# Attention and two MLPs on one core: score products in float32 from the loaded rows, and a new order of the attention round

## The chip, the cores and the metric

The kernel runs on one core of a Trainium2 chip. The metric is the time of one execution on the device in microseconds (us); three runs of the kernel before gave 993.02, 993.51 and 996.86, so the median is 993.51.

## The reference

```python
# attention: q, k, v of 4 batches x 8 heads x 576 tokens x 64, f of 4 x 8 x 576
scores = scale * np.matmul(q, k.transpose(0, 1, 3, 2))
cum = np.cumsum(np.log(np.clip(f, 0.0001, 1.0)), axis=-1)
scores = np.where(causal, -1e9, scores + cum[..., :, None] - cum[..., None, :])
attn = np.exp(scores - np.max(scores, axis=-1, keepdims=True))
x = np.matmul(attn / (np.sum(attn, axis=-1, keepdims=True) + 1e-09), v)
# x as 2304 tokens x 512, then two MLPs
h = x @ w_in;  x = (h * np.cos(h)) @ w_out          # 512 -> 2048 -> 512
g = x @ w_gate                                      # 512 -> 1536
x = (g / (1 + np.exp(-g)) * (x @ w_val)) @ w_out2   # 1536 -> 512
```

The weights come as 64-bit floats, and the kernel converts them itself.

## The kernel before, in words

The kernel has an attention stage and then two MLP stages. The change touches attention alone (and the point in it where two products of the first MLP are put ahead).

The 32 heads are worked in 16 pairs. The pair's q and k lie as 128 rows (two heads of 64 dimensions) by 2 x 576 tokens in a tile `raw`, loaded by `load_pair`. Queries are cut into tiles: tile t = 0 to 3 holds 128 queries against their first 128(t+1) keys, for each head; tile 4 holds the last 64 queries of both heads against all 576 keys, with q laid on the diagonal of a block `bd` so that one product serves both. For every pair the order has these operations, named by a letter and the tile (and, where there is one for each head, by a last digit 0 or 1):

- **q0 to q3** (`emit_q`, POOL): q and k rounded to float32r (high part), and what is left (low part), in `xq`. **qb** (`emit_b`, POOL): the blocks `bd` and `sf`.
- **S** (`emit_s`, TensorE): scores. Three products (high x high, low x high, high x low) and one more that adds the decay from `cs`. The two heads use the upper and the lower 64 rows of the array. Pair 0, and pair 1 but for tiles 1 and 4, take one product of the loaded rows instead, in float32, with block `bd0` for pair 0's tile 4. A float32 product is issued as two instructions.
- **M** (`emit_m`, DVE): mask, scale, maximum, from PSUM into `P` (tile 4: `Q`). **E** (`emit_e`, ACT): exponential and row sum.
- **T** (`emit_t`, TensorE): `P` transposed in blocks of 64 into a PSUM tile `t` (two buffers, shared with V). **C** (`emit_c`): that tile copied into `pt`, on ACT or DVE. For groups 0 to 2 the two heads' halves are copied apart, and `CPD` names those that DVE takes.
- **V** (`emit_pv`, TensorE, float32): the product with v, in two halves, 28 instructions. **N** (`emit_n`, DVE): times the reciprocal sums. **xo**: the store of the result to DRAM.
- **r**: the reciprocals of the sums: `ra` (POOL), `rb` (DVE), `rt` (transpose), `rc` (copy on ACT), `rd` (store), `re`, `rf` (loads of the broadcast rows `rs`).
- **w1 to w7** (`w_step`): one weight tile's conversion: w1 ACT, w2 POOL (line 170, a clamp), w3 DVE (line 172, a shift), w4 and w5 DVE (lines 174, 176), w6 POOL (a rounding), w7 POOL (line 115, a subtraction). **wd**, **ld**, **lv** are loads of a weight tile, a pair, and v. **xk** loads and splits the first chunk of MLP input.

`SCH` is the order of a round, written out by hand: an entry such as `V0@3` runs operation V0 of pair n-3 in round n. The rounds n = 0, 1, ... follow each other, and the entries of pairs out of range are left out, so the first and last rounds are partly empty. `in_order` ties each engine to this order: an engine starts nothing before what stands ahead of it on the same engine. `FIRST` gives pairs 0 and 1 another order of score tiles; `AHEAD` moves a few reciprocal steps of pairs 0 and 1. `XH` names the two places where twelve products of the first MLP (`ahead`, `mm_in`, line 253) are put ahead of an attention operation. After the last round the first MLP's loop runs; its input chunk 1 is fetched behind a `gate` (a one-element copy on DVE, line 144).

In PSUM the scores of tiles 0, 2 and 4 share `sA` and those of tiles 1 and 3 `sB` (`SAT`), one buffer each, so a tile's scores wait for the maxima of the one before in the same place.

Of the kernel before, what the change touches and what calls it, by code (L numbers as in the profile page):

```python
# [9 lines left out]
F32 = mybir.dt.float32  # L10
F32R = mybir.dt.float32r
# [7 lines left out]
B, H, S, D = 4, 8, 576, 64  # L19
NH = B * H  # L20
NPAIR = NH // 2
# [8 lines left out]
SA = 15  # L30
LAG = 2
PB = 6
RWB = 3
VTB = 3
PTB = 2
PST = 2
# [5 lines left out]
CHAIN = 1  # L42
WHE = 1

CPD = ("10", "11", "21")
FIRST = {0: "20314", 1: "32041"}
XH = {("T1", NPAIR - 1): 0, ("V0", NPAIR - 1): 1}
SCH = "M21@2 w4@4 M31@2 q2@0 w5@4 N0@4 E30@2 ld@-1 N1@4 S4@1 T1@3 E00@2 re@3 rf@3 q0@0 S1@1 xo@4 wd@2 E01@2 E10@2 M40@1 w6@4 T3@3 E21@2 E31@2 C10@3 S2@1 C11@3 w1@3 ra@2 S0@1 w2@3 q3@0 rb@2 M10@1 M11@1 T2@3 rt@2 C30@3 w3@3 q1@0 qb@0 C21@3 E40@1 T0@2 S3@1 rc@2 C20@3 rd@2 M20@1 M01@1 M00@1 C01@2 M30@1 V0@3 E11@1 V1@3 E20@1 w7@4 lv@2 C00@2 xk@3"
JS = 9
NCH = 96  # L50
NPASS, NQ, NST = 3, 6, 2
# [31 lines left out]
PJ = [0, 576, 1088, 1408, 1024]  # L83
# [14 lines left out]
def body(ctx: ExitStack, tc: tile.TileContext, qk, v, f, w_in, w_out, w_gate, w_val, w_out2, mask_c, ident_c, sel_c, out):  # L98
    nc = tc.nc
    PE, ACT, DVE, POOL, SP = nc.tensor, nc.scalar, nc.vector, nc.gpsimd, nc.sync  # L100
# [13 lines left out]
    def subtract(eng, o, a, b):  # L114
        eng.tensor_tensor(out=o, in0=a, in1=b.bitcast(F32), op=ALU.subtract)  # L115

    def pool_round(o, a):
        POOL.tensor_scalar(out=o, in0=a, scalar1=1.0, scalar2=0.0, op0=ALU.mult, op1=ALU.add)
# [161 lines left out]
    ap1 = actx.enter_context(tc.tile_pool(name="ap1", bufs=1))  # L280
# [3 lines left out]
    aps = actx.enter_context(tc.tile_pool(name="aps", bufs=1))  # L284
# [13 lines left out]
    raws = {}  # L298

    def load_pair(i):  # L300
        raws[i] = aps.tile([128, 2, S], F32, tag="raw", name="raw", bufs=RWB)
        SP.dma_start(out=raws[i], in_=qk[i])
# [7 lines left out]

    Ps = [ap1.tile([128, PW], F32, name=f"P{k}") for k in range(PB)]
    P4s = [ap1.tile([128, 640], F32, name=f"Q{k}") for k in range(PB // 2)]
    bd = [ap1.tile([128, 2, 128], F32R, name=f"bd{k}") for k in range(2)]
    sel = ap1.tile([128, NPAIR, 2], F32R, name="sel")
    sel4s = [ap1.tile([128, 128], F32R, name=f"sf{k}") for k in range(2)]
    bd0 = ap1.tile([128, 128], F32, name="bd0")
    fo, lc = Ps[2:4]
    lf, ones, cum = fo[:, 0:S], fo[:, S:2 * S], lc[:, 0:S]
    cs = aps.tile([128, S], F32R, name="cs")
    selr = aps.tile([128, NPAIR + 1], F32, name="selr")  # L320
    POOL.memset(mask[:, 0:384], 0.0)
    POOL.memset(mask4[:, 0:512], 0.0)
    for b in (bd0, sel, *bd):
        POOL.memset(b.bitcast(F32), 0.0)
    SP.dma_start(out=lf, in_=f)
    load_pair(0)
    SP.dma_start(out=selr, in_=sel_c)
# [32 lines left out]

    SAT = {0: (sA, 384), 1: (sB, 0), 2: (sA, 0), 3: (sB, 0)}

    xq = {}

    def emit_q(i, k):

        if i not in xq:
            xq[i] = aps.tile([128, 2, 2, S], F32R, tag="xq", name="xq", bufs=2)
        h, l, x = xq[i][:, 0, k // 2], xq[i][:, 1, k // 2], raws[i][:, k // 2]
        if k % 2 == 0:  # L370
            pool_round(h, x)
        else:
            subtract(POOL, l, x, h)

    def emit_b(i):
        q = slice(512, S)
        if i == 0:
            for e in range(2):
                b = slice(64 * e, 64 * e + 64)
                pool_round(sel[b, :, e], selr[b, :NPAIR])  # L380
        pool_round(sel4s[i % 2].rearrange("p (e x) -> p e x", e=2), sel[:, i, :, None].bitcast(F32).to_broadcast([128, 2, 64]))
        for e in range(2):
            b = slice(64 * e, 64 * e + 64)
            if i:
                pool_round(bd[i % 2][b, :, b], xq[i][b, :, 0, q].bitcast(F32))
            else:
                pool_round(bd0[b, b], raws[i][b, 0, q])

    early = {}

# [8 lines left out]
        return x[:, :, lo:lo + QT[t][1]]  # L399

    def emit_s(i, t):
        if i > 1 or i == 1 and t in (1, 4):
            xh, xl = xq[i][:, 0], xq[i][:, 1]
            h, l = bd[i % 2][:, 0], bd[i % 2][:, 1]
            p = (xh, xh, h), (xl, xh, l), (xh, xl, h)
        else:
            p = (raws[i], raws[i], bd0),
        if t < 4:
            q0, ext, _ = QT[t]
            o = s_place(i, t)  # L410
            for m, (x, y, _) in enumerate(p):
                for e in range(2):
                    b = slice(64 * e, 64 * e + 64)
                    PE.matmul(o[:, e], lhsT=x[b, 0, q0:q0 + 128], rhs=y[b, 1, :ext], start=(m == 0), stop=False)
            for e in range(2):
                b = slice(64 * e, 64 * e + 64)
                PE.matmul(o[:, e], lhsT=sel[b, i, e:e + 1].to_broadcast([64, 128]), rhs=cs[b, :ext], start=False, stop=True)
            return
        o = s_place(i, 4)
        for m, (x, y) in enumerate([*((x, y) for _, y, x in p), (sel4s[i % 2], None)]):  # L420
            for g in range(2):
                k = slice(288 * g, 288 * g + 288)
                PE.matmul(o[:, g], lhsT=x, rhs=cs[:, k] if y is None else y[:, 1, k], start=(m == 0), stop=(y is None))

    P = {}
    mxt = [ap1.tile([128, 5], F32, name=f"mx{i}") for i in range(8)]
# [65 lines left out]
            for h in range(2):  # L492
                turn(ps[:, h, 64 * n:64 * n + 64], x, h)

    def emit_c(i, g, e):
        if i not in PT:
            PT[i] = ap2.tile([128, 2, PTW], F32, tag="pt", name="pt", bufs=PTB)
        ps, o = tps[i, g], PT[i]

        def copy(o, x):  # L500
            if f"{g}{e}" in CPD or i == 0 and g == 3:
                DVE.tensor_copy(o, x)
            else:
                ACT.copy(out=o, in_=x)  # L504

        n = 4 - g
        if g < 3:
            copy(o[:, e, PJ[g]:PJ[g] + 128 * n].rearrange("p (n h x) -> p n h x", n=n, h=2),
                 ps[:, :, 64 * n * e:64 * n * e + 64 * n].rearrange("p h (n x) -> p n h x", n=n))
            return  # L510
        if g == 3:
            copy(o[:, :, PJ[g]:PJ[g] + 128].rearrange("p e (h x) -> p e h x", h=2), ps[:, :, :128].rearrange("p h (e x) -> p e h x", e=2))
            c = 128
            for js in TAILS:
                a, k = PJ[js[0]] + KW[js[0]] - 64, len(js)
                d = PJ[js[1]] + KW[js[1]] - 64 - a
                copy(o[:, :, a:a + d * (k - 1) + 64].rearrange("p e (j q) -> p e j q", q=64)[:, :, ::d // 64],
                     ps[:, :, c:c + 64 * k].rearrange("p e (j q) -> p e j q", j=k))
                c += 64 * k
# [39 lines left out]
    SLOTS = {k: [t for _, _, t in sorted((int(f), n, t) for n, (t, f) in enumerate(sch) if t[0] == k)] for k in "SME"}  # L559
# [4 lines left out]
    def op(o, i):  # L564

        if not 0 <= i < NPAIR:
            return
        if i in FIRST and o[0] in "SME":
            o = o[0] + flat(o[0], FIRST[i])[SLOTS[o[0]].index(o)]
        if (o, i) in BEHIND:  # L570
# [2 lines left out]
            act(*a)  # L573
        act(o, i)

    AHEAD = {("M10", 1): (("ra", 0), ("rb", 0)), ("C10", 0): (("rt", 0), ("rc", 0), ("rd", 0)), ("T0", 1): (("re", 0), ("rf", 0))}
    BEHIND = {a for b in AHEAD.values() for a in b}

    def act(o, i):
        k, e = o[0], int(o[-1]) if o[-1] in "01" else 0  # L580
        p = 2 * i + e
        if o[:2] == "ld":
            i > 1 and load_pair(i)
        elif o == "lv":
            prep_v(i)
        elif k == "S":
            emit_s(i, int(o[1]))
        elif k == "M":
            emit_m(p, int(o[1]))
        elif k == "E":  # L590
            emit_e(p, int(o[1]))
        elif k == "T":
            emit_t(i, int(o[1]))
        elif k == "C":
            emit_c(i, int(o[1]), e)
        elif k == "r":
            emit_recip(i, o[1])
        elif k == "V":
            emit_pv(i, e)
        elif k == "N":  # L600
            emit_n(i, e)
        elif o == "xo":
            emit_o(i)
        elif o == "xk":
            if i == XL:
                load_chunk(0, True)
            elif i >= XP:
                for _ in range(min(XN, len(xsplit))):
                    split_x(*xsplit.pop(0))
        elif o == "wd":  # L610
            i and w_load(i - 1)
        elif k == "w":
            i and w_step(i - 1, int(o[1]))
        elif o == "qb":
            emit_b(i)
        elif k == "q":
            i and emit_q(i, int(o[1]))
        else:
            raise ValueError(o)

# [18 lines left out]
    for n in range(NPAIR + moff):  # L639
        for o, off in sch:  # L640
            if (o, n - int(off)) in XH:
                ahead(XH[o, n - int(off)])
            op(o, n - int(off))
            if n - int(off) == NPAIR - 1 and o == "C01":
                ACT.activation(out=sinp, in_=hpi, func=AF.Sin)
    in_order(first)
    gsrc[0] = const.tile([1, 1], F32, name="gs")
# [131 lines left out]
    for i in range(NCH + LAG):  # L779
        if i < NCH:  # L780
            g, j = steps[i]
            c, a, b = SEG[g]
# [60 lines left out]
    ps = ctx.enter_context(tc.tile_pool(name="ps", bufs=1, space=PSUM, reuse_waits="tile"))  # L843
# [182 lines left out]
    for st in range(NST):  # L1026
        for p in range(NPASS):
            final = st == NST - 1 and p == NPASS - 1
            for q in range(NQS * st, NQS * st + NQS):
                k = q - NQS * st  # L1030
# [89 lines left out]
```

## Time and profile before

| | |
|---|---|
| median of three runs | 993.51 us |
| the profiled execution's own time | 992.61 us |
| its span, first to last instruction | 990.5 us |
| TensorE (PE) busy | 949.6 us, 96% |
| DVE busy | 747.9 us, 76% |
| ACT busy | 502.2 us, 51% |
| POOL busy | 496.8 us, 50% |
| granted TensorE clock, mean | 0.989 |

The profile is one execution. Busy times are those of instructions that work on data. A matmul's end is modelled, so a busy PE need not be at its peak. The shares are means over the attention stage (0 to about 191 us) and the MLP stages after it.

### The profile page before, as it was taken

The page shows a single profiled execution, that of the slowest core. Times are in us where ns is not written, and L with a number is a line of the kernel's source. Part 1 is how long each engine was busy: PE and PEld are TensorE (multiplying, and loading weights), DVE is VectorE, ACT ScalarE, POOL GpSimd, SP SyncE. Part 2 cuts the span into 40 slices and gives each one's busy share as a digit, 9 for nine tenths or more (in the row PEclk, how much of TensorE's full clock was granted, in tenths as well). Part 3 has the DMA queues.
Part 4 walks back from the last instruction along what each step waited for, and adds up shares of the span by engine and source line. Part 5 has one row for each costly group of instructions (what it writes and reads, how often), then busy time and mean ns, then how long its engine had stood idle before and what let it go on. Part 6 is the DMA issues. An engine that isn't in the chain of part 4 may idle for free.

```text
span 990.5 us, 18044 instructions
## 1 busy us (share of the span) xinstructions
PE 949.6 (96%) x6522; PEld 897.8 (91%) x6522; DVE 747.9 (76%) x1312; ACT 502.2 (51%) x1106; POOL 496.8 (50%) x492
## 2 busy tenths in 40 slices
PE   7898887799999999999999999999999999999998
PEld 4676675699999999999999999999999999988888
DVE  6888987378788878879894744867567686898884
ACT  6787786355555555556655532423233241454552
POOL 6699997352227569679785002644454464200000
PEclk9999998989999999999999999999999999999999
DMA  5565564333356767877856775134951419953431
GB/s 171 185 217 194 187 220 135 136 105 129 94 193 206 243 201 236 268 236 260 278 195 223 258 265 171 48 120 133 341 182 49 127 50 352 347 195 125 147 107 43
DMA packets 108984, 182.60 MB, mean 184 GB/s; under 512 B 8912, under 2 KB 72800, under 8 KB 108896
## 3 DMA queue, kind: packets, MB, share of 16 engines
q1 hardware_dynamic: 108896, 181.46, 55.6%
q8 instruction: 51, 0.84, 0.3%
q14 instruction: 37, 0.30, 0.1%
HBM read 118.43 MB, written 62.99 MB: 183 GB/s over the span
## 4 chain that ended last, share of the span: by engine, by line
PE 72%; DVE 3%; issue 2%; POOL 2%; DMA 1%; ACT 0%; SPq 0%; DVEq 0%; POOLq 0%; ACTq 0%
PE h L253 17%; PE t L699 16%; PE b L890 11%; PE c L890 8%; PE a L890 8%; PE b L979 5%; PE a L979 3%; PE c L979 1%; PE d L979 1%; PE t L702 1%; DVE c L115 1%; DMA xl<-x 1%; POOL sums L115 1%; DVE gs L764 0%; DVE ta L174 0%
## 5 line engine op out<-in xcount | busy, mean ns | idle before, releaser
L253 PE MATMUL h<-xh,w 128*128 128x384 f32 x768 | 150.0, 336 | 0.0
L699 PE MATMUL t<-gh,w 128*128 128x384 f32 x704 | 137.9, 337 | 4.1 <-ACT gh L683 3.5
L253 PEld LDWEIGHTS h<-xh,w 128*128 128x128 f32 x768 | 135.5, 189 | 0.2
L699 PEld LDWEIGHTS t<-gh,w 128*128 128x128 f32 x704 | 124.1, 189 | 5.1 <-ACT gh L683 3.8
L890 PE MATMUL b<-c,wu 128*128 128x384 f32 x648 | 121.1, 334 | 0.0
L675 ACT ACTIVATE n<-h 128x384 int32<-128x384 f32 x96 | 47.2, 491 | 139.9 <-PE h L253 139.7
L890 PEld LDWEIGHTS b<-c,wu 128*128 128x128 f32 x648 | 113.1, 188 | 0.0
L677 DVE SCALAR_TENSOR_TENSOR r<-h,n 128x384 f32<-128x384 f32 x96 | 53.1, 553 | 73.5 <-ACT n L675 73.2
L853 POOL TENSOR_TENSOR s<-u,s 128x384 f32<-128x384 f32 x33 | 37.7, 1144 | 123.7 <-ACT s L852 123.7
L253 PE MATMUL h<-xl,w 128*128 128x384 f32 x384 | 82.0, 334 | 0.0
L890 PE MATMUL c<-c,wu 128*128 128x384 f32 x432 | 80.7, 334 | 0.0
L890 PE MATMUL a<-c,wu 128*128 128x384 f32 x432 | 80.7, 334 | 0.0
L115 POOL TENSOR_TENSOR w<-ta,w 128x512 fp32r<-128x512 f32 x32 | 48.8, 1524 | 62.4 <-DVE ta L172 31.3
L699 PE MATMUL t<-gl,w 128*128 128x384 f32 x352 | 75.8, 336 | 0.0
L890 PEld LDWEIGHTS c<-c,wu 128*128 128x128 f32 x432 | 75.4, 188 | 0.0
L890 PEld LDWEIGHTS a<-c,wu 128*128 128x128 f32 x432 | 75.4, 188 | 0.0
L533 PEld LDWEIGHTS t<-pt,vt 128*64 128x64 f32 x448 | 32.0, 147 | 46.8 <-ACT pt L504 28.6
L533 PE MATMUL t<-pt,vt 128*64 128x320 f32 (+4 forms) x448 | 51.7, 386 | 22.7 <-ACT pt L504 22.6
L446 ACT ACTIVATE P<-P,mx 128x256 f32<-128x256 f32 (+3 forms) x128 | 70.2, 550 | 0.2 <-DVE mx L438 0.2
L253 PEld LDWEIGHTS h<-xl,w 128*128 128x128 f32 x384 | 67.9, 188 | 0.0
L172 DVE TENSOR_SCALAR ta<-ta 128x512 int32<-128x512 int32 x68 | 56.3, 828 | 14.3 <-POOL ta L170 13.8
L679 ACT ACTIVATE r<-r,hpi 128x384 f32<-128x384 f32 x96 | 59.5, 619 | 10.6 <-DVE r L677 10.5
(160 smaller groups left out, 2122.9 us busy)
## 6 DMA issues: line engine op xcount, KB each, us to landing
wu<-wu SPq DMA_DIRECT2D x63, 512.0 KB, 7.7
wraw<-in_w_out_dram SPq DMA_DIRECT2D x28, 512.0 KB, 3.8
wu<-hi SPq DMA_DIRECT2D x54, 256.0 KB, 4.4
gd<-g SPq DMA_DIRECT2D x72, 192.0 KB, 2.3
gt<-gd SPq DMA_DIRECT2D x36, 384.0 KB, 3.9
raw<-in_qk_dram SPq DMA_DIRECT2D x16, 576.0 KB, 4.4
wu<-sums SPq DMA_DIRECT2D x36, 256.0 KB, 4.3
xb<-x SPq DMA_DIRECT2D x24, 384.0 KB, 5.8
```

Source lines behind the costliest of these rows:

```text
L115: eng.tensor_tensor(out=o, in0=a, in1=b.bitcast(F32), op=ALU.subtract)
L172: DVE.tensor_scalar(out=ta, in0=ta, scalar1=5, scalar2=2, op0=ALU.logical_shift_left, op1=ALU.logical_shift_right)
L253: PE.matmul(ps, lhsT=w[:, a, 128 * kk:128 * kk + 128], rhs=b[:, kk], start=(n == 0), stop=(n == 3 * KD - 1))
L446: ACT.activation(out=o, in_=o, func=AF.Exp, scale=-1.0, bias=mxt[p % 8][:, t:t + 1], accum_out=smt[p // 2 % 3][:, c:c + 1])
L533: PE.matmul(ps[64 * e:64 * e + 64, o:min(w, o + KW[j])], lhsT=vt_t[i][:, j, e], rhs=PT[i][:, e, c:c + w - o], start=(j == 0), stop=(j == b ...
L675: ACT.activation(out=n, in_=h, func=AF.Copy, scale=INV2PI, bias=0.25)
L677: DVE.scalar_tensor_tensor(out=r, in0=h, scalar=INV2PI, in1=n, op0=ALU.mult, op1=ALU.subtract)
L679: ACT.activation(out=r, in_=r, func=AF.Sin, bias=hpi, scale=float(2 * np.pi))
L699: PE.matmul(acc[m][:, :CH], lhsT=wo[:, q, 128 * m:128 * m + 128], rhs=x, start=(j == a and n == 0), stop=False)
L853: e.tensor_tensor(out=s, in0=C[:, 0], in1=s, op=ALU.mult)
L890: PE.matmul(d, lhsT=wu[q, i][1][:, mem, x, 128 * kt:128 * kt + 128], rhs=r, start=bool(s and n == 0), stop=(n == 5), skip_group_check=True)
L979: PE.matmul(ot[:, :w], lhsT=cmb[i][:, x, q], rhs=m[:, 256 * y:256 * y + w], start=(i in (1, 5) and n == 0), stop=(n == len(ops) - 1), skip ...
```

## The change

The split of q and k goes (`emit_q`, `xq`, the low and high `bd`): all pairs take one float32 product of the loaded rows for each score tile, and `bd` is now float32, filled from the loaded rows. `emit_c` copies both heads in one operation; DVE takes group 1 (and pair 0's group 3), ACT the rest. The loaded pairs get a fourth buffer (`RWB`). The round has a new order, in which V, N and xo stand at the head of a round with offset 4, and w6, w7 have offset 5; pair 1's order of score tiles, the places of `AHEAD` and `XH` and the place of the sine table's load move with it.

```diff
-RWB = 3
+RWB = 4
...
-CPD = ("10", "11", "21")
-FIRST = {0: "20314", 1: "32041"}
-XH = {("T1", NPAIR - 1): 0, ("V0", NPAIR - 1): 1}
-SCH = "M21@2 w4@4 M31@2 q2@0 w5@4 N0@4 E30@2 ld@-1 N1@4 S4@1 T1@3 E00@2 re@3 rf@3 q0@0 S1@1 xo@4 wd@2 E01@2 E10@2 M40@1 w6@4 T3@3 E21@2 E31@2 C10@3 S2@1 C11@3 w1@3 ra@2 S0@1 w2@3 q3@0 rb@2 M10@1 M11@1 T2@3 rt@2 C30@3 w3@3 q1@0 qb@0 C21@3 E40@1 T0@2 S3@1 rc@2 C20@3 rd@2 M20@1 M01@1 M00@1 C01@2 M30@1 V0@3 E11@1 V1@3 E20@1 w7@4 lv@2 C00@2 xk@3"
+FIRST = {0: "20314", 1: "20341"}
+XH = {("V0", NPAIR - 2): 0, ("V0", NPAIR - 1): 1}
+SCH = "lv@3 E21@2 V0@4 E30@2 V1@4 M31@2 qb@0 w6@5 w4@4 N0@4 N1@4 xo@4 E01@2 C0@3 ld@-1 S4@1 E31@2 S1@1 re@3 rf@3 M40@1 w7@5 T3@3 w5@4 T1@3 ra@2 wd@2 w1@3 M11@1 C3@3 rb@2 M10@1 S0@1 w2@3 C1@3 S2@1 E11@1 T2@3 rt@2 M00@1 E10@1 M21@1 M20@1 w3@3 S3@1 C2@3 rc@2 rd@2 T0@2 M30@1 E00@1 E40@1 E20@1 xk@3 M01@1"
...
-    bd = [ap1.tile([128, 2, 128], F32R, name=f"bd{k}") for k in range(2)]
+    bd = [ap1.tile([128, 128], F32, name=f"bd{k}") for k in range(2)]
...
-    xq = {}
-
-    def emit_q(i, k):
-
-        if i not in xq:
-            xq[i] = aps.tile([128, 2, 2, S], F32R, tag="xq", name="xq", bufs=2)
-        h, l, x = xq[i][:, 0, k // 2], xq[i][:, 1, k // 2], raws[i][:, k // 2]
-        if k % 2 == 0:
-            pool_round(h, x)
-        else:
-            subtract(POOL, l, x, h)
-
...
-            if i:
-                pool_round(bd[i % 2][b, :, b], xq[i][b, :, 0, q].bitcast(F32))
-            else:
-                pool_round(bd0[b, b], raws[i][b, 0, q])
+            pool_round(bd[i % 2][b, b], raws[i][b, 0, q])
...
     def emit_s(i, t):
-        if i > 1 or i == 1 and t in (1, 4):
-            xh, xl = xq[i][:, 0], xq[i][:, 1]
-            h, l = bd[i % 2][:, 0], bd[i % 2][:, 1]
-            p = (xh, xh, h), (xl, xh, l), (xh, xl, h)
-        else:
-            p = (raws[i], raws[i], bd0),
+        x = raws[i]
         if t < 4:
             q0, ext, _ = QT[t]
             o = s_place(i, t)
-            for m, (x, y, _) in enumerate(p):
-                for e in range(2):
-                    b = slice(64 * e, 64 * e + 64)
-                    PE.matmul(o[:, e], lhsT=x[b, 0, q0:q0 + 128], rhs=y[b, 1, :ext], start=(m == 0), stop=False)
+            for e in range(2):
+                b = slice(64 * e, 64 * e + 64)
+                PE.matmul(o[:, e], lhsT=x[b, 0, q0:q0 + 128], rhs=x[b, 1, :ext], start=True, stop=False)
...
-        for m, (x, y) in enumerate([*((x, y) for _, y, x in p), (sel4s[i % 2], None)]):
+        for m in range(2):
             for g in range(2):
                 k = slice(288 * g, 288 * g + 288)
-                PE.matmul(o[:, g], lhsT=x, rhs=cs[:, k] if y is None else y[:, 1, k], start=(m == 0), stop=(y is None))
+                if m:
+                    PE.matmul(o[:, g], lhsT=sel4s[i % 2], rhs=cs[:, k], start=False, stop=True)
+                else:
+                    PE.matmul(o[:, g], lhsT=bd[i % 2], rhs=x[:, 1, k], start=True, stop=False)
...
-    def emit_c(i, g, e):
+    def emit_c(i, g):
...
-            if f"{g}{e}" in CPD or i == 0 and g == 3:
+            if g == 1 or i == 0 and g == 3:
                 DVE.tensor_copy(o, x)
             else:
                 ACT.copy(out=o, in_=x)
 
         n = 4 - g
         if g < 3:
-            copy(o[:, e, PJ[g]:PJ[g] + 128 * n].rearrange("p (n h x) -> p n h x", n=n, h=2),
-                 ps[:, :, 64 * n * e:64 * n * e + 64 * n].rearrange("p h (n x) -> p n h x", n=n))
-            return
+            copy(o[:, :, PJ[g]:PJ[g] + 128 * n].rearrange("p e (n h x) -> p e n h x", n=n, h=2),
+                 ps[:, :, :128 * n].rearrange("p h (e n x) -> p e n h x", n=n, e=2))
...
-    AHEAD = {("M10", 1): (("ra", 0), ("rb", 0)), ("C10", 0): (("rt", 0), ("rc", 0), ("rd", 0)), ("T0", 1): (("re", 0), ("rf", 0))}
+    AHEAD = {("M40", 1): (("ra", 0), ("rb", 0)), ("C3", 0): (("rt", 0), ("rc", 0), ("rd", 0)), ("T2", 0): (("re", 0), ("rf", 0))}
...
-            if n - int(off) == NPAIR - 1 and o == "C01":
+            if n - int(off) == NPAIR - 1 and o == SLOTS["E"][-1]:
                 ACT.activation(out=sinp, in_=hpi, func=AF.Sin)
```

## Rows read from the trace of the kernel before

**Rows 1.** The page, busy us, share of the span and instructions of TensorE.

```profile
PE 949.6 (96%) x6522; PEld 897.8 (91%) x6522; DVE 747.9 (76%) x1312; ACT 502.2 (51%) x1106; POOL 496.8 (50%) x492
```

**Rows 2.** Windows: stretch, length, busy (count) by engine, granted clock, DMA share, GB/s.

```profile
18.29:158.10 139.81, 116.43 (x1562) 92.31 (x1562) 119.84 (x350) 105.74 (x344) 124.49 (x141) 0.98 0.61 199
158.10:191.03 32.93, 27.13 (x302) 21.29 (x299) 21.00 (x51) 17.75 (x49) 17.80 (x18) 0.90 0.36 119
191.03:990.50 799.47, 791.99 (x4579) 776.09 (x4578) 594.86 (x862) 364.89 (x678) 341.24 (x305) 1.00 0.57 186
```

**Rows 3.** Timeline of SP's queue: start, us, result stores of two successive pairs.

```profile
83.34 0.33 SPq L547 DMA_DIRECT2D x<-xp  x1
...
93.79 0.33 SPq L547 DMA_DIRECT2D x<-xp  x1
```

**Rows 4.** Windows: one round, columns PE, PEld, DVE, ACT, POOL as in rows 2.

```profile
83.34:93.79 10.45, 8.60 (x126) 6.91 (x124) 9.32 (x28) 8.07 (x28) 9.95 (x12) 1.00 0.62 201
```

**Rows 5.** Timeline of DVE: start, us, w3 beside a busy and an idle POOL.

```profile
86.80 1.63 DVE L172 TENSOR_SCALAR ta<-ta 128x512 int32<-128x512 int32 x1 [1.13 <-POOL ta L170]
...
183.07 0.41 DVE L172 TENSOR_SCALAR ta<-ta 128x512 int32<-128x512 int32 x1
```

**Rows 6.** Timeline of PE: the first V instructions of a round, idle before.

```profile
89.36 0.87 PE L533 MATMUL t<-pt,vt 128*64 128x256 f32 x8 [1.85 <-ACT pt L504]
```

**Rows 7.** Groups of POOL by form, 50 to 150 us: count, busy us, mean ns, idle.

```profile
L115 POOL TENSOR_TENSOR xq<-raw,xq 128x576 fp32r<-128x576 f32 x18 | 26.6, 1501 | 0.0
...
L118 POOL TENSOR_SCALAR xq<-raw 128x576 fp32r<-128x576 f32 x20 | 17.1, 868 | 0.0
...
L118 POOL TENSOR_SCALAR bd<-xq 64x128 fp32r<-64x128 f32 x18 | 5.3, 294 | 0.7
```

**Rows 8.** Groups of DVE and ACT by form, 50 to 150 us: the copies of transposed scores.

```profile
L502 DVE COPY pt<-t 128x384 f32<-128x384 f32 x20 | 10.1, 544 | 0.0
...
L502 DVE COPY pt<-t 128x256 f32<-128x256 f32 x9 | 3.7, 410 | 0.0
...
L504 ACT COPY pt<-t 128x256 f32<-128x256 f32 x29 | 10.3, 355 | 1.6 <-PE t L483 1.6
L504 ACT COPY pt<-t 128x512 f32<-128x512 f32 x18 | 10.1, 563 | 0.0
```

**Rows 9.** Timeline of PE: tile 4 and tile 3 of a late pair, three rounded products.

```profile
81.75 1.06 PE L423 MATMUL sA<-xq,bd 128*128 128x288 f32 x6
...
82.65 0.42 PE L423 MATMUL sA<-cs,sf 128*128 128x288 f32 x2
...
86.33 0.95 PE L414 MATMUL sB<-xq 64*128 64x512 f32 x6
...
87.12 0.40 PE L417 MATMUL sB<-cs,sel 64*128 64x512 f32 x2
```

**Rows 10.** The same tiles of pairs 0 and 1, one float32 product.

```profile
9.34 1.24 PE L423 MATMUL t<-raw,bd 128*128 128x288 f32 x4
...
10.20 0.64 PE L423 MATMUL t<-cs,sf 128*128 128x288 f32 x2
...
10.78 1.13 PE L414 MATMUL sB<-raw 64*128 64x512 f32 x4
...
11.34 0.80 PE L417 MATMUL sB<-cs,sel 64*128 64x512 f32 x2
```

**Rows 11.** Timeline of PE: three V products, 28 instructions each.

```profile
153.56 4.61 PE L533 MATMUL t<-pt,vt 128*64 128x256 f32 x28 [2.45 <-ACT pt L504]
...
164.09 2.92 PE L533 MATMUL t<-pt,vt 128*64 128x256 f32 x28 [0.20 <-ACT pt L504]
...
174.35 4.47 PE L533 MATMUL t<-pt,vt 128*64 128x256 f32 x28 [2.40 <-ACT pt L504]
```

**Rows 12.** Windows: a stretch of the first MLP, where PE has only rounded 384-column products.

```profile
225.00:250.00 25.00, 25.00 (x146) 25.00 (x145) 21.63 (x40) 14.34 (x30) 5.42 (x4) 1.00 0.40 129
```

**Rows 13.** Timeline of PE: tile 4 of pair 2, idle before.

```profile
18.29 1.06 PE L423 MATMUL sA<-xq,bd 128*128 128x288 f32 x6 [2.61 <-POOL bd L118]
```

**Rows 14.** Timeline of DVE: the gate of the second MLP chunk.

```profile
197.66 0.14 DVE L144 CAST xl<-gs 1x1 fp32r<-1x1 f32 x1 [6.66 <-issue]
```

More of the change, by code (lines that the diff above doesn't have):

```diff
@@ L312, in body @@
     P4s = [ap1.tile([128, 640], F32, name=f"Q{k}") for k in range(PB // 2)]
-    bd = [ap1.tile([128, 2, 128], F32R, name=f"bd{k}") for k in range(2)]
+    bd = [ap1.tile([128, 128], F32, name=f"bd{k}") for k in range(2)]
     sel = ap1.tile([128, NPAIR, 2], F32R, name="sel")
     sel4s = [ap1.tile([128, 128], F32R, name=f"sf{k}") for k in range(2)]
-    bd0 = ap1.tile([128, 128], F32, name="bd0")
     fo, lc = Ps[2:4]
@@ L322, in body @@
     POOL.memset(mask4[:, 0:512], 0.0)
-    for b in (bd0, sel, *bd):
-        POOL.memset(b.bitcast(F32), 0.0)
+    for b in (sel.bitcast(F32), *bd):
+        POOL.memset(b, 0.0)
     SP.dma_start(out=lf, in_=f)
@@ L594, in act @@
         elif k == "C":
-            emit_c(i, int(o[1]), e)
+            emit_c(i, int(o[1]))
         elif k == "r":
@@ L615, in act @@
             emit_b(i)
-        elif k == "q":
-            i and emit_q(i, int(o[1]))
         else:
```

## The prediction

> **What bounds the kernel now.** I first read the page's engine totals: TensorE is busy for 96% of the span [rows 1]. Such a share is a mean over stages, so I cut the span where the stages change. After 191.03 us (the last attention result leaves) TensorE is busy 791.99 of 799.47 us [rows 2]: the two MLPs run at its pace, nothing in the change touches them, and I cost them at nothing. Everything is decided in the 191 us of attention before.
>
> There the work comes in rounds. The stores of the attention results leave 10.45 us apart [rows 3], and in one such round POOL is busy 9.95 us, DVE 9.32, PE 8.60, ACT 8.07 [rows 4]. POOL has half a microsecond left in twelve instructions, which is their own starting time, so POOL sets the round. The others show that they wait for it: DVE idles 1.13 us for POOL's clamp ahead of its shift (w3), that shift then lasts 1.63 us beside POOL's subtractions where it lasts 0.41 us beside an idle POOL [rows 5], the copy behind it comes late, and PE idles 1.85 us for the copies of the transposed scores ahead of the V product [rows 6]. That is one chain: POOL, DVE, ACT, PE.
>
> **The change, part by part.**
>
> *No split of q and k (POOL).* Per round POOL loses two roundings at 0.868 and two subtractions at 1.501 us: 4.74 us [rows 7]. The block for the last 64 queries stays two operations, on 64x64 in place of 64x128 (0.294 us each [rows 7]); I keep their price. POOL falls from 9.95 to 5.2 us a round and cannot pace a round above that. What it slowed gets quicker too: DVE's shift may fall from 1.63 towards 0.41 us [rows 5], but POOL still has its clamp and its weight subtraction each round, so I bound DVE's gain here between 0 and 1.2 us.
>
> *Copies of both heads in one operation.* DVE had two copies of 384 columns and one of 256: 2 x 0.544 + 0.410 = 1.50 us. It keeps one of 768. From 256 to 384 columns a copy grows by 0.134 us [rows 8], so 768 come to 0.544 + 3 x 0.134 = 0.95 us: DVE saves 0.55. ACT had two of 512 and one of 256 (2 x 0.563 + 0.355 = 1.48 us) and gets one of 1024 and one of 512; 256 columns more cost 0.208 us [rows 8], so 0.563 + 2 x 0.208 + 0.563 = 1.54: ACT gains 0.06. No row has the new pattern, which runs over both heads and has one dimension more. By the nearest rows it lies between these sums and the price of the separate copies it joins plus half as much again (DVE +0.7, ACT +0.8); I take the sums, since the inner run stays 64 columns. So DVE goes from 9.32 to 7.6 to 8.8 us a round, ACT from 8.07 to 8.1.
>
> *Scores as float32 products (PE).* Per round three products of rounded parts (six matmuls for a tile) become one float32 product (four instructions for a tile, since float32 is issued as two for each head). Pairs 0 and 1 already do this in the trace, so the same tiles stand there in both forms. Measured from the first start to the last end with the decay product behind it, the last-queries tile took 81.75 to 82.65 + 0.42, so 1.32 us, and in float32 9.34 to 10.20 + 0.64, so 1.50; the 512-column tile 86.33 to 87.12 + 0.40, so 1.19, and in float32 10.78 to 11.34 + 0.80, so 1.36 [rows 9, 10]. That is +0.18 and +0.17. The other three are shorter, where two instructions fewer weigh most: I take nothing for them. Sum +0.35 us a round. The upper end comes from columns alone: the float32 V product runs 1600 columns in 2.92 us, or 1.82 ns a column [rows 11], the MLP's rounded products 384 columns in 25.00/146 = 0.171 us, 0.446 ns a column [rows 12]. The round's 1280 + 576 score columns would go from 3 x 0.446 to 1.82 ns: +0.9 us. The lower end is 0, if fewer instructions win back the columns. So PE needs 8.60 + 0.35 = 8.95 us a round, between 8.6 and 9.5.
>
> In "FP8 and Floating Point Precision", section "TensorE Precision Notes", the Trainium skill says that true FP32 takes four passes through the array; that speaks against this edit, since three products become four passes. The trace agrees on the rate (1.82 against 0.446 ns a column), while the tiles' elapsed times show less than half of the rise. With four passes paid in full the round would be 9.5 us.
>
> *Round laid out anew.* The order decides whether PE really gets to run through. I walked one round by it, with durations from these rows, V starting at 0. V ends at 2.9; the division (DVE) runs to 3.7; the last-queries scores end at 4.4 and their maximum at 5.1; w5, the two 256-column maxima and a reciprocal end at 6.5 to 7.0; ACT's exponentials of these end at 7.5 and its last copy and row copy at about 8.1. Only these hold the next V, and PE itself is busy to 8.95. The shift w3 now stands behind the copy that V needs, so POOL's clamp holds no copy for PE: the 1.85 us [rows 6] go. ACT's own loop, 8.1 us and half a microsecond of wait for the last 512-column maxima, also fits. What is late next is PE itself. I take 9.0 us a round. On SP the pair's load now stands behind the result's store, which waits for the division; it leaves by about 4.5 and is used in the next round. A fourth buffer of loaded rows lets it leave without waiting for readers.
>
> **The sum**, against the profiled execution (span 990.50, time 992.61 us).
> - Middle: from the last-queries scores of pair 2 (18.29) to those of pair 15 (158.10) are 13 rounds and 139.81 us [rows 2]. Thirteen rounds of 10.45 would be 135.9; the remaining 4 us are two V products that ran long, beside a mean granted clock of 0.98 (one took 4.61 in place of 2.92 us, [rows 11]). PE with fewer idle gaps should keep the clock. New: 13 x 9.0 = 117.0. Saved 22.8.
> - Start: pair 2's scores waited 2.61 us for the block that POOL builds from the rounded parts [rows 13]; that block now comes from the loaded rows. The maxima of pair 1 are over by then, so the wait goes whole; the first rounds, still without V, may be a little shorter than 9.0. Saved 3.3 (bounds 1 to 5).
> - End: from 158.10 to the last V product's results, 32.93 us at a granted clock of 0.90 [rows 2], in rounds without score work but with the same chain through w3, and with one more slow V (4.47 us at 174.35, [rows 11]). By the walk: 6 us to end round 16; 8.8 for the next, where the table load for the sine and the exponentials are in ACT's way; about 12.7 to the end of the last V, with two groups of twelve MLP products ahead of it; 1 for division and store. 28.5 us. Saved 4.4 (bounds 1 to 7).
> - Seam: DVE stood idle for 6.66 us until 197.66 [rows 14], after the last store and before the second chunk of MLP input is fetched; that hangs behind the store and moves with it. Nothing saved.
>
> Sum 30.5 us: 992.61 - 30.5 = 962.1. The median of the runs shown, 993.51, lies 0.9 above the profiled time, so I predict 963.
>
> **Rivals.**
> - *DVE and ACT pace the round* (20%): the joined copies cost their upper end, DVE's shift still stands beside POOL's subtractions, and the two hand each other waits: DVE 8.8 + 0.7, so 9.6 us a round. Middle 139.8 - 124.8 = 15, start 2, end 3: 973. For it: today's 9.32 and 8.07 are no small loads. Against: POOL's share halves.
> - *Float32 costs its full columns* (9%): 9.5 us a round, 16.3 + 3 + 4 saved: 970. For it: the V product's rate [rows 11]. Against: [rows 9, 10]. This is what the Trainium skill's four passes would make of it.
> - *PE pays nothing more* (8%): the loads of two matmuls fewer win back the columns, 8.6 a round, 28 + 4.5 + 6 saved: 955.
> - *The gain doesn't come* (3%): a wait in the new order (V for the last copy, which waits for the exponentials of maxima that wait for w5) takes the 1.85 us' place and the round stays near 10.3; start and end give a few microseconds: 990.
> - *Slower* (3%): the granted clock. If the new order leaves PE idle at the wrong places, the array runs at 1.2 GHz of its 2.4 for much of the round. The slow V product was 4.61/2.92 = 1.58 times as long, so a round wholly at the low level costs 9.0 x 1.58 = 14.2 us and the time is 1030. It decides from the point where 13 x (9.0 + 5.2 f) passes 139.8 + 7.7, so f = 0.45 of the rounds. Against: such slow stretches stood behind idle PE only, and the change takes idle time away.
>
> The forecast itself holds 57%, with its own range 957 to 969. To hold 8 in 10 I reach from 952 (the cheap end) to 980 (the DVE and ACT case with short savings at both ends). A measurement of this kernel can tell about 0.5%, 5 us, from no change: faster by more 94%, within 3%, slower 3%.
>
> **What would show it.** Right: stores of results about 9.0 us apart; POOL near 5.2 us busy in such a distance, PE without an idle gap ahead of V; pair 2's last-queries scores at about 15.5 us in place of 18.29; the last store at about 160 us; the MLP span unchanged near 799.5. Wrong: stores over 9.4 us apart with PE idle behind DVE or ACT (first rival), or with PE solid (second); a granted clock under 0.95 in the middle; an MLP part that grows by more than 2 us.

## The result and the profile after

The changed kernel takes 968.91 us (median of four runs, 967.03 to 970.48) against 995.18 us for the kernel before (four runs): a ratio of 0.9734, 95% interval 0.9699 to 0.9769. The profiled execution took 967.03 us over a span of 965.3 us; before it was 992.61 over 990.5. So the spans differ by 25.2 us, where the forecast had 30.5.

These are the windows of the changed kernel, cut at the same events as [rows 2] (pair 2's last-queries scores, pair 15's, the last store), once more from pair 3's scores to pair 15's, and over one round as in [rows 4]; the columns are length, then busy us (count) of PE, PEld, DVE, ACT and POOL, the granted clock, the DMA share and GB/s.

```profile
16.19:134.33 118.14, 117.43 (x1436) 86.57 (x1433) 100.43 (x327) 108.38 (x330) 63.34 (x86) 1.00 0.71 216
26.40:134.33 107.93, 107.93 (x1324) 79.83 (x1321) 93.68 (x299) 99.43 (x302) 62.60 (x83) 1.00 0.75 230
134.33:165.47 31.14, 27.20 (x294) 21.07 (x290) 18.90 (x47) 18.99 (x47) 15.56 (x15) 0.95 0.36 114
165.47:965.30 799.83, 791.20 (x4578) 774.54 (x4576) 593.59 (x863) 364.78 (x678) 343.31 (x307) 1.00 0.57 187
81.34:90.33 8.99, 8.99 (x113) 6.65 (x111) 7.55 (x25) 8.23 (x26) 5.02 (x7) 1.00 0.74 229
```

The last line tells the change: in a round POOL went from 9.95 to 5.02 us, and PE is busy in all of its 8.99 us. The first, third and fourth give the account against [rows 2]: start 18.29 to 16.19 (2.1 saved), middle 139.81 to 118.14 (21.7), end 32.93 to 31.14 (1.8), MLPs 799.47 to 799.83 (0.4 lost).

The timeline of PE in the same round (start, us) answers to [rows 6, 9 and 10]: the last-queries tile, the 128-column tile (and the start of the next), the 512-column tile, and the next V, which starts with no idle time before it where 1.85 us stood. Behind it two lines of SP's queue, the stores of two successive pairs, which answer to [rows 3].

```profile
80.37 1.24 PE L403 MATMUL sA<-raw,bd 128*128 128x288 f32 x4
81.23 0.64 PE L401 MATMUL sA<-cs,sf 128*128 128x288 f32 x2
...
83.26 0.44 PE L391 MATMUL sA<-raw 64*128 64x128 f32 x4
...
83.60 0.86 PE L391 MATMUL sA<-raw 64*128 64x384 f32 x4
...
84.77 1.08 PE L391 MATMUL sB<-raw 64*128 64x512 f32 x4
85.28 0.80 PE L394 MATMUL sB<-cs,sel 64*128 64x512 f32 x2
...
86.51 2.92 PE L512 MATMUL t<-pt,vt 128*64 128x256 f32 x28
```

```profile
81.34 0.34 SPq L526 DMA_DIRECT2D x<-xp  x1
...
90.33 0.34 SPq L526 DMA_DIRECT2D x<-xp  x1
```

From pair 3 to pair 15 the last-queries scores are 107.93 us apart (26.40 to 134.33), 8.99 us a round over twelve, and PE is busy in all of it (second line of the windows).

DVE and ACT by form between 50 and 140 us (count, busy us, mean ns) show the joined copies, which answer to [rows 8], and w3, which answers to [rows 5]:

```profile
L482 DVE COPY pt<-t 128x768 f32<-128x768 f32 x10 | 9.5, 948 | 0.0
...
L171 DVE TENSOR_SCALAR ta<-ta 128x512 int32<-128x512 int32 x10 | 4.8, 481 | 0.0
...
L484 ACT COPY pt<-t 128x1024 f32<-128x1024 f32 x10 | 9.8, 985 | 0.0
...
L484 ACT COPY pt<-t 128x512 f32<-128x512 f32 x10 | 5.9, 586 | 0.0
```

The copies cost what the slope of the shorter ones said (0.95 and 0.98 us), and the shift costs 0.48 us on average, near its 0.41 beside an idle POOL.

### The profile page after: what moved, and what is told of

Its sections match the earlier page's. It is cut to its first block, busy times and chain, and to the rows that moved or that the text cites. A ratio compares the mean times of both kernels' runs of the same rounds, so it can differ in the third digit from the quotient of the medians.

```text
span 965.3 us, 17642 instructions
## 1 busy us (share of the span) xinstructions
PE 949.7 (98%) x6378; PEld 890.2 (92%) x6378; DVE 724.7 (75%) x1280; ACT 504.8 (52%) x1090; POOL 427.6 (44%) x431
## 4 chain that ended last, share of the span: by engine, by line
PE 84%; DVE 5%; ACT 3%; POOL 3%; DMA 3%; issue 2%; SPq 0%; DVEq 0%; POOLq 0%; ACTq 0%
PE h L252 16%; PE t L676 15%; PE b L867 12%; PE c L867 8%; PE a L867 8%; PE b L956 5%; PE t L512 4%; PE a L956 3%; PE t L463 2%; PE sB L391 2%; PE sA L403 2%; PE c L956 2%; PE d L956 2%; DMA xl<-x 1%; ACT P L426 1%
## 5 line engine op out<-in xcount | busy, mean ns | idle before, releaser
L114 POOL TENSOR_TENSOR w<-ta,w 128x512 fp32r<-128x512 f32 x32 | 45.2, 1414 | 59.6 <-ACT w L189 31.9
L426 ACT ACTIVATE P<-P,mx 128x384 f32<-128x384 f32 (+3 forms) x128 | 70.6, 555 | 1.2 <-DVE mx L418 1.2
L173 DVE SCALAR_TENSOR_TENSOR ta<-wraw,ta 128x512 int32<-128x512 int32 x68 | 67.1, 987 | 0.6
L676 PEld LDWEIGHTS t<-gl,w 128*128 128x128 f32 x352 | 62.6, 189 | 0.0
L956 PE MATMUL b<-wu,c 128*128 128x256 f32 (+1 forms) x342 | 61.4, 329 | 0.2 <-DVE u L741 0.2
```

The costliest lines, as they stand in the source:

```text
L173: DVE.scalar_tensor_tensor(out=ta, in0=lo, scalar=29, in1=ta, op0=ALU.logical_shift_right, op1=ALU.bitwise_or)
L426: ACT.activation(out=o, in_=o, func=AF.Exp, scale=-1.0, bias=mxt[p % 8][:, t:t + 1], accum_out=smt[p // 2 % 3][:, c:c + 1])
L676: PE.matmul(acc[m][:, :CH], lhsT=wo[:, q, 128 * m:128 * m + 128], rhs=x, start=(j == a and n == 0), stop=False)
L956: PE.matmul(ot[:, :w], lhsT=cmb[i][:, x, q], rhs=m[:, 256 * y:256 * y + w], start=(i in (1, 5) and n == 0), stop=(n == len(ops) - 1), skip ...
```

## The experiments

The theory: POOL's split set the round before, PE sets it now, DVE and ACT lie under it. What fell short of the forecast was to be looked for at the two ends. All times below are medians; the ratios are to the kernel before on the same chip.

**Only the split taken out.** The order, copies and places of the kernel before; four buffers of loaded rows.

```diff
# in the kernel before
-RWB = 3
+RWB = 4
...
-        p = (xh, xh, h), (xl, xh, l), (xh, xl, h)      # raws only for pair 0 and part of pair 1
+        p = (raws[i], raws[i], bd[i % 2]),             # all pairs; q0 to q3 emit nothing
```

> The order, copies and places of before, with only the split of q and k gone: float32 products of the loaded rows for all pairs, four buffers of loaded rows. Theory (POOL's split set the round before; the new order only takes away the wait that is then left): POOL near 5.2 us busy a round, the stores of results 9.3 to 9.5 us apart with PE idle 0.3 to 0.5 us ahead of V, time about 972. Rival (the new order carries the gain): stores 10.0 us apart or more, PE idle over 1 us a round, time 980 or more.

Measured: 976.78 us, ratio 0.9812 (0.9793 to 0.9832). Windows from pair 3's to pair 15's last-queries scores, a timeline of DVE's w3 and of PE's V in one of its rounds:

```profile
31.03:141.34 110.31, 108.38 (x1324) 77.78 (x1321) 93.21 (x324) 96.66 (x305) 62.03 (x86) 1.00 0.67 218
```

```profile
90.85 0.43 DVE L172 TENSOR_SCALAR ta<-ta 128x512 int32<-128x512 int32 x1 [1.06 <-POOL ta L170]
...
92.21 2.92 PE L512 MATMUL t<-pt,vt 128*64 128x256 f32 x28 [0.23 <-ACT pt L483]
```

110.31 us over twelve rounds is 9.19 us a round. The shift still waits 1.06 us for POOL's clamp, but it lasts 0.43 us in place of 1.63, and PE's idle time ahead of V falls from 1.85 to 0.23 us. So the split's removal alone carries 18 of the 26 us, and without the split even the old order keeps almost nothing of the old chain. The time is 5 us over what the theory gave, and that lies ahead of this window: pair 3's scores start at 31.03, against 26.40 in the changed kernel. In that start PE waits 2.05 us for a reciprocal and 1.34 us for a copy, and runs at a mean granted clock of 0.76 from 17 to 31 us. This is what the new order mostly brings: 4.6 us in the first rounds, 0.2 us in each later one, and 3.3 us behind them (from pair 15's scores to the last store 31.14 us in the changed kernel, 34.44 here).

**The split put back into the new order**, written by POOL and read by nobody. `emit_q` comes back for it, with one buffer for what it writes.

```diff
# two places in SCH
-w7@5
+w7@5 q0@0 q1@0
...
-w2@3
+w2@3 q2@0 q3@0
```

> The changed kernel, with POOL's two roundings and two subtractions put back in each round; nobody reads what they write. Theory (POOL's work sets the round when the split is there): POOL 10 us busy a round and a round of 10.2 to 10.5 us, time 984 to 988. Rival (the new order hides POOL's work): round stays near 9.0, time within 3 us of the changed kernel's 969.

Measured: 985.64 us, ratio 0.9909 (0.9888 to 0.9929). Windows over an early round, in which POOL has the split but not yet the whole weight conversion, and over a later one:

```profile
36.70:45.70 9.00, 9.00 (x115) 6.66 (x111) 8.29 (x25) 8.08 (x26) 8.35 (x11) 1.00 0.76 230
76.11:86.72 10.61, 9.39 (x114) 6.68 (x111) 7.61 (x25) 8.39 (x27) 9.94 (x11) 1.00 0.68 192
```

In the later rounds POOL is back at 9.94 us and the round at 10.5 (84.03 us for eight rounds from 55.24 to 139.27). In the early one POOL has 8.35 us of work, and the round is 9.00 us with PE busy throughout: here the split costs time only where POOL's work is longer than PE's. This and the run before show the cause from both sides. With the split in it the kernel is still 9 us faster than before; its later rounds are as long as before, so that part lies at the start, in the early rounds and at the end.

**The price of the float32 product.** Two kernels in which POOL rounds q and k (1.7 us a round, off the path) and pairs 2 to 15 use the rounded rows: once for a lower bound, three times for the old split's work on TensorE. The second of these comes first here; "the one before" in its text is the other.

```diff
-                PE.matmul(o[:, e], lhsT=x[b, 0, q0:q0 + 128], rhs=x[b, 1, :ext], start=True, stop=False)
+            for m in range(w):      # w = 1 or 3; x = q and k rounded to float32r
+                ...
+                    PE.matmul(o[:, e], lhsT=x[b, 0, q0:q0 + 128], rhs=x[b, 1, :ext], start=(m == 0), stop=False)
```

> As the one before, but the product of the rounded rows is taken three times into the same place (scores come out three times too large), so TensorE does the work of the old split without POOL's subtractions. It prices the float32 product. If float32 costs 0.35 us a round more than three rounded products: PE 8.65 us a round, the round 8.65 to 8.75 with PE solid, time 964 to 966. If it costs its columns (0.9): PE 8.1 a round with 0.5 us idle, the round at ACT's 8.6, time 963 to 964. If it costs nothing: 9.0 a round with PE solid, time 969.

Measured: 962.57 us, ratio 0.9671 (0.9651 to 0.9691). A window over one round, and PE's timeline at its 128-column tile and the next:

```profile
77.74:86.31 8.57, 8.57 (x124) 7.08 (x120) 7.78 (x25) 8.33 (x27) 7.69 (x11) 1.00 0.76 241
```

```profile
80.34 0.53 PE L400 MATMUL sA<-xq 64*128 64x128 f32 x6
...
80.82 0.74 PE L400 MATMUL sA<-xq 64*128 64x384 f32 x6
```

PE is solid here too, and the round is 8.58 us (94.39 us for eleven). So float32 costs 8.99 - 8.58 = 0.41 us a round against three rounded products, close to the 0.35 taken and far from the 0.9 of its columns. The shortest tile shows where the rest goes: from its start to the start of the next, the 128-column tile takes 0.34 us in float32 (83.26 to 83.60 above) and 0.48 us as six rounded instructions (80.34 to 80.82). The last-queries and 512-column tiles cost 0.18 and 0.13 us more in float32, counted the same way.

> The changed kernel, but pairs 2 to 15 take one product of the rounded rows (POOL rounds q and k, 1.7 us a round); the low parts are left out, so scores are less exact. PE's round loses about 2.5 us of column time. Theory (PE sets the round at 9.0, ACT is next at 8.55 us busy): the round falls to 8.6 or 8.7, not further, PE idle over 1.5 us a round, time 963 to 965. Rival (DVE and ACT set the round already): round stays at 9.0, time 968 to 970.

Measured: 960.58 us, ratio 0.9651 (0.9628 to 0.9674). A window over the ten rounds from pair 3 to pair 13:

```profile
26.10:107.24 81.14, 72.98 (x1004) 52.96 (x1000) 75.72 (x249) 81.12 (x250) 65.21 (x87) 1.00 0.81 250
```

The round falls further than I wrote, to 8.11 us, and ACT is busy in 81.12 of 81.14 us. The expectation used 8.55 us for ACT, from a window of 9.30 us, longer than a round; the forecast's own 8.1 was right. So PE sets the round at 9.0, and ACT is next at 8.1.

**Copies apart, and three buffers.**

```diff
-            copy(o[:, :, PJ[g]:PJ[g] + 128 * n].rearrange("p e (n h x) -> p e n h x", n=n, h=2),
-                 ps[:, :, :128 * n].rearrange("p h (e n x) -> p e n h x", n=n, e=2))
+            for e in range(2):
+                copy(o[:, e, PJ[g]:PJ[g] + 128 * n].rearrange("p (n h x) -> p n h x", n=n, h=2),
+                     ps[:, :, 64 * n * e:64 * n * e + 64 * n].rearrange("p h (n x) -> p n h x", n=n))
```

> The changed kernel, with the copies of the transposed scores of groups 0 to 2 made for each head apart again, on the same engines (DVE 2 x 384, ACT 2 x 512 and 2 x 256 columns). Theory (PE sets the round at 9.0; DVE and ACT lie under it): DVE +0.1, ACT +0.2 us busy a round, the round stays at 9.0 within 0.05, time within 2 us of 969. Rival (copies are part of what sets the round): 0.2 us or more a round, time 972 or more.

Measured: 968.53 us, ratio 0.9727 (0.9703 to 0.9751).

```diff
-RWB = 4
+RWB = 3
```

> The changed kernel with three buffers of loaded rows in place of four. Theory (the load of a pair is used a round later; PE never waits for it): the load in the rounds still finds a free buffer, since the oldest pair's scores are done; only the first loads move, time 968 to 970. Rival (the load waits for the scores of the pair before, and holds SP's queue): POOL's block and then PE wait, 0.3 us a round or more, time 973 or more.

Measured: 968.60 us, ratio 0.9730 (0.9704 to 0.9756). Neither part of the change moves the time in the new order beyond the spread of the runs: both lie under PE.

**The end of attention.** Here the forecast had 28.5 us and the trace 31.1. A timeline of the changed kernel (start, us, engine) shows a chain that starts with the load of the sine table:

```profile
144.74 1.28 ACT L622 ACT_TABLE_LOAD   x1
...
146.15 0.65 ACT L167 ACTIVATE ta<-wraw 128x512 f32<-128x512 f32 x1
...
146.69 1.01 ACT L484 COPY pt<-t 128x256 f32<-128x256 f32 x3
...
147.75 0.46 PE L463 MATMUL t<-ident,P 64*128 64x64 f32 x8 [2.67 <-ACT pt L484]
...
148.70 2.95 PE L252 MATMUL h<-xh,w 128*128 128x384 f32 x8
...
148.88 0.75 POOL L117 TENSOR_SCALAR xh<-xl 128x384 fp32r<-128x384 f32 x1
...
149.68 1.46 PEld L252 LDWEIGHTS h<-xh,w 128*128 128x128 f32 x5 [0.51 <-POOL xh L117]
...
151.45 1.41 PE L252 MATMUL h<-xl,w 128*128 128x384 f32 x4
...
157.81 1.66 PE L252 MATMUL h<-xh,w 128*128 128x384 f32 x8
```

The table stands ahead of w1 and of three copies, and PE waits 2.67 us for the last of these. Of the eight products at 148.70, which take 2.95 us against 1.66 at 157.81, three go through; then the weight loads wait 0.51 us for POOL's last split of the chunk. The other five and the four at 151.45 run at about half speed: the mean granted clock from 149.68 to 152.78 is 0.52, near the lower of its two levels (1.2 of 2.4 GHz). Two edits follow from it:

```diff
-            if n - int(off) == NPAIR - 1 and o == SLOTS["E"][-1]:
+            if n - int(off) == NPAIR - 1 and o == "C0":
                 ACT.activation(out=sinp, in_=hpi, func=AF.Sin)
```

> The changed kernel, with the load of the sine table on ACT moved from behind the last exponential to behind the next round's copy of group 0. Theory (the end was 2.6 us longer than forecast because the 1.28 us load delays w1, the copies of group 3 and so PE's transposes): PE's wait of 2.67 us there falls to about 1.2, the twelve MLP products ahead start about 1.5 us earlier but still wait for POOL's last split of the chunk; 1 to 2 us less, time 967 to 968. Rival (POOL's chain w1, w2, split holds the end all the same): no change, 969.

Measured: 967.23 us, ratio 0.9712 (0.9690 to 0.9734). PE's timeline at the same places:

```profile
146.21 0.46 PE L463 MATMUL t<-ident,P 64*128 64x64 f32 x8 [1.15 <-ACT pt L484]
...
148.16 1.78 PE L252 MATMUL h<-xh,w 128*128 128x384 f32 x5 [0.22 <-POOL xh L117]
```

PE's wait falls to 1.15 us, as the theory had it, and the wait for POOL's split stays. The five products behind that still run at half speed (1.78 us), at a granted clock of 0.50 from 149 to 151: the long wait isn't needed for that.

```diff
# and, beside the edit above
-XN = 1
+XN = 2
```

> As the one before, and two splits of the first MLP chunk in a round, so that all four are done two rounds before the products ahead. Theory: these products wait for nothing and PE's clock stays up; 3 to 4 us less than the changed kernel, time 965 to 966. Rival (only one of the two causes counts): same as the run before.

Measured: 964.89 us, ratio 0.9697 (0.9671 to 0.9724). PE's timeline:

```profile
146.70 0.46 PE L463 MATMUL t<-ident,P 64*128 64x64 f32 x8 [1.16 <-ACT pt L484]
...
147.65 1.66 PE L252 MATMUL h<-xh,w 128*128 128x384 f32 x8
```

The eight products now take 1.66 us at a granted clock of 1.00, behind as long a wait for the copy (1.16 us), and the last store leaves at 163.18 in place of 165.47. Between the two of them the edits give back about 3 to 4 us (span 965.3 to 962.2, median 968.91 to 964.89); each single step is within the spread of the runs, the traces show it place by place.

**The seam.** Behind the last store PE waits again in the changed kernel, as it did before (first line, of the kernel before), but for another reason. A timeline of POOL, DVE, SP, ACT and PE:

```profile
198.84 2.93 PE L699 MATMUL t<-gh,w 128*128 128x384 f32 x8 [3.47 <-ACT gh L683]
```

```profile
166.84 1.29 POOL L114 TENSOR_TENSOR w<-ta,w 128x512 fp32r<-128x512 f32 x1
...
167.84 0.14 DVE L143 CAST xl<-gs 1x1 fp32r<-1x1 f32 x1 [1.79 <-DMA x<-xp]
...
168.15 0.34 SPq L151 DMA_DIRECT2D wraw<-in_w_in_dram  x1
...
171.86 0.66 ACT L167 ACTIVATE ta<-wraw 128x512 f32<-128x512 f32 x1 [9.58 <-DMA wraw<-in_w_in_dram]
...
173.32 2.93 PE L676 MATMUL t<-gh,w 128*128 128x384 f32 x8 [3.67 <-ACT gh L660]
```

The gate (167.84) passes 2.4 us after the store's issue at 165.47, where it took 6.6 before (191.03 to 197.66, [rows 14]). But the next weight tiles' loads leave only when POOL's last w7 is done, and ACT stands behind the first of them. So I moved the last w5 ahead of the last division (run e8):

```diff
-        if (o, i) in BEHIND:
+        if (o, i) in BEHIND or (o, i) == ("w5", NPAIR - 1):
             return
...
         act(o, i)
+        if (o, i) == ("w4", NPAIR - 1):
+            act("w5", i)
```

> As the one before, and the last weight tile's w5 on DVE directly behind its w4, ahead of the last division. Theory (behind attention, ACT idles 9.6 us for a weight tile whose loads wait for POOL's last w7, which waits for this w5 behind the last division; PE then idles 3.7 us and its clock falls): the loads leave about 4 us earlier, PE's wait falls below 1.5 us, 3 to 5 us less, time 961 to 963. Rival (the gate behind the last store holds the same place): at most 1 us less.

Measured: 965.86 us, ratio 0.9704 (0.9683 to 0.9725), no better than the 964.89 before it: the rival. The first load does leave at 161.6, but now the store stands behind four of them, and the gate passes only 6.6 us after it again. The profile names no releaser for the gate here; that it waits for the store is inferred, and the next run tries it:

```profile
163.45 0.40 SPq L526 DMA_DIRECT2D x<-xp  x1
...
170.04 0.14 DVE L143 CAST xl<-gs 1x1 fp32r<-1x1 f32 x1 [7.13 <-issue]
...
171.22 2.93 PE L678 MATMUL t<-gh,w 128*128 128x384 f32 x8 [4.11 <-ACT gh L662]
```

Then only two loads went ahead of the store (run e9):

```diff
-            if i == 0:
-                for n in range(RWB2):
-                    w_load(SA + n)
+            for n in {0: range(2), 3: range(2, RWB2)}.get(i, ()):
+                w_load(SA + n)
```

> As e8, but of the four weight loads behind attention only two are issued ahead of the last store; the other two come behind the load of the second chunk. Theory (in e8 the store landed 6.6 us after its issue because four loads of 512 KB stood ahead of it in the queues, and the gate waited for it; without loads ahead it lands 2.4 us after): the store lands 4 to 5 us after its issue, the gate passes near 168, PE's wait behind attention falls from 4.1 to about 2 us, 2 to 3 us less than e8, time 963. Rival (the store waits for something else): gate still 6.5 us behind the store, time 965 to 966.

Measured: 963.34 us, ratio 0.9680 (0.9657 to 0.9702), the fastest version that keeps float32 scores:

```profile
164.40 0.33 SPq L526 DMA_DIRECT2D x<-xp  x1
...
168.62 0.14 DVE L143 CAST xl<-gs 1x1 fp32r<-1x1 f32 x1 [4.25 <-DMA x<-xp]
...
169.80 1.66 PE L678 MATMUL t<-gh,w 128*128 128x384 f32 x8 [1.22 <-ACT gh L662]
```

The gate passes 4.2 us behind the store's issue, with the store named as what released it; PE waits 1.22 us, and the products after it run at full speed. Against 964.89 the gain of 1.5 us is within the spread of the runs.

The last run joins this with the one rounded product, e4 in its text.

> As e9, with the one rounded product of e4 for pairs 2 to 15 (the low parts are left out). Theory: the gains add, since e4's lies in the rounds (8.13 us, ACT busy throughout) and e9's behind them: 960.6 less 5 to 6, time 954 to 956. Rival (with rounds set by ACT, the end of attention is set by ACT too, and the seam edits bring less): 957 or more.

Measured: 958.35 us, ratio 0.9637 (0.9611 to 0.9663). The edits bring 2.2 us here, not 5 to 6. Its windows from pair 2's scores to pair 15's and behind the last store, and PE's V in the longest round:

```profile
16.25:129.72 113.47, 98.74 (x1307) 70.98 (x1303) 96.71 (x327) 107.03 (x328) 84.16 (x113) 0.97 0.72 225
159.16:955.90 796.74, 789.94 (x4578) 773.03 (x4576) 596.42 (x862) 365.15 (x678) 342.45 (x305) 1.00 0.57 187
```

```profile
117.97 4.32 PE L521 MATMUL t<-pt,vt 128*64 128x256 f32 x28 [2.60 <-DMA vt<-in_v_dram]
```

Behind the last store the gain is there: 796.74 us, where e4 has 802.53. But the rounds take 113.47 us against e4's 109.32; in one of them, 11.79 us long, V waits 2.60 us for the load of v and then runs long. So the rival's reason (the end set by ACT) is not what the trace shows. These are single executions, and why that load came late was not tried.

## Why the prediction was right, and where it was short

The forecast was 963, the time 968.91: well inside the range of 952 to 980, and inside the narrower one, 957 to 969, by 0.1 us. The saving was 25.2 us in place of 30.5. Step by step:

- **What bounds the kernel** held: POOL, shown by taking the split away and by putting it back. The half microsecond that POOL had left in a round was not all starting time: 0.17 us of it was a wait for ACT at the clamp.
- **A round of 9.0 us set by PE** held: 8.99. So did POOL's 5.2 (5.02), ACT's 8.1 (8.23) and DVE's fall to the low end of 7.6 to 8.8 (7.55). The float32 products cost 0.41 us a round, taken as 0.35; the bound from columns, 0.9, is refuted as a price of the edit: about half of it is won back. That the removed instructions do this fits the 128-column tile, which got shorter by 0.14 us; no run varied their number alone. The three shorter tiles, taken at nothing, come to +0.05 us together. The copies in a pattern over both heads cost what the slope gave (the upper bound on ACT, +0.8, would be +1.2 by its own rule; nothing came of it). The four passes that the Trainium skill states for true FP32 ("FP8 and Floating Point Precision", section "TensorE Precision Notes") would give the 0.9; the trace agrees with them on the rate of the columns, not on the price of this edit.
- **Start**: 2.1 us saved, taken as 3.3. I wrote that pair 1's maxima are over by then. They are not: the 256-column scores of pair 1 wait 0.33 us for DVE to free `sB`, and pair 2's tile starts behind them at 16.19 in place of 15.5. That wait is about half of the 0.7 us; PE is busy in the rest. The first interval behind it is 10.21 us, not shorter than 9.0 (PE waits there 0.30 us for a copy and 0.41 us for a reciprocal); that is the 1.1 us by which the middle fell short.
- **End**: the term that was most off. 1.8 us saved, taken as 4.4. The round with the sine table took 8.2 us (140.47 to 148.70), taken as 8.8. The last piece, from there to the end of the last V, took 15.8 us (148.70 to 164.51), taken as 12.7. Two things were mis-sized. The twelve products ahead took 4.1 us behind PE's wait and the split (148.70 to 152.78), where they take 2.2 when neither is there; and nine further products of the next tile stood ahead of the last V (160.00 to 161.65, 1.7 us), which I had not counted. The kernel before already had seven there (1.3 us, from 185.90 to 187.21), so its trace could have told.
- **Seam**: nothing saved, as forecast, but not because it "moves with the store". One wait went (the gate), and another of the same size took its place (ACT behind the weight load). That was right by luck.

Of the rivals, "DVE and ACT pace the round" needed 9.6 us a round, and full columns 9.5; the round was 8.99 with PE busy throughout, and ACT alone allows 8.11. The granted clock did what the slower rival feared, but only at the ends (0.95 over the last 31 us), not in the rounds.

## What to carry to other kernels

Find the engine that is busy for all but its starting costs in one period of the loop, not in the whole span; taking its work away moves the period down to the next engine and no further, so the gain is the distance to that one (10.45 to 9.0 here, with 8.1 behind it). An extra third of TensorE's column time cost less than half of what its columns say here, in an edit that also removed instructions, and rows of the same operation in both forms, even from a prologue, price it better than its columns. Ends of a phase don't shrink with its rounds: walk them with every instruction that stands in the queue, and look at which transfer stands ahead of which.

## What was not expected of the hardware

- The gate behind the last store passed 2.4 us after the store's issue with no load ahead of it, 4.2 with two loads of 512 KB ahead, 6.6 with four. In the first two the profile names the store as the releaser; in the last that is inferred.
- DVE's shift takes 1.63 us beside POOL's subtractions of 576 columns and 0.43 when these are gone (old order without the split), though it starts right behind the same POOL clamp in both.
- The granted clock fell to its lower level behind waits of different length. In the changed kernel PE had idled 2.67 us for the copies, and the clock was 0.52 from 149.68 to 152.78. With the sine table moved PE had idled 1.15 us, then 0.22 for the split, and the clock fell all the same (0.50 from 149 to 151). With the split earlier too PE had idled 1.16 us, without the second wait, and the clock stayed at 1.00 from 147.65 to 149.93. These are single executions; the length of the one wait does not tell the cases apart.
